# Blocks of 512 tokens with single buffers in the FFN of an attention and mixture-of-experts kernel, and unread products in its first wait

## The chip, the cores and the metric

The kernel runs on one core of a Trainium2 chip. The metric is device time in microseconds (us), the median of several executions. One further execution was taken by the hardware profiler; the rows below are from it. TensorE does the matmuls (PE in rows, PEld its weight loads), VectorE is DVE, ScalarE is ACT, GpSimd is POOL, SyncE (SP) issues transfers.

## The reference

Linear attention without a softmax, an RMS norm, a mixture of eight experts with one expert for each token, and a bilinear FFN over all 2304 tokens:

```python
kv = np.einsum('bhsd,bhse->bhde', k, v)            # (4, 8, 64, 64)
out = np.einsum('bhsd,bhde->bhse', q, kv)          # (4, 8, 576, 64)
x = out / sqrt(mean(out * out) + 1e-6) * g_norm    # as (2304, 512)
e = argmax(x @ w_gate)                             # top-1 of 8, capacity 576
y = relu(x @ w1[e]) @ w2[e]                        # 512 -> 1024 -> 512
out = gate * y
a = out @ w1_ ; b = out @ w2_                      # 512 -> 1024 each
result = ((a * b) @ w3) @ w_out                    # 1024 -> 1024 -> 512
```

## The kernel before

**Precision.** Every large product is done with operands split into a rounded part "hi" and a remainder "lo". PASSES lists three matmuls, hi x hi, hi x lo and lo x hi, so a product over 512 rows (KC = 4 chunks of 128) takes 12 matmuls and one over 1024 rows takes 24.

**Attention and gate** (to about 86 us). For each of four batches: kv, the products with q, norm, gate logits, and the ranks of tokens within their expert. At its end `emit_gather(0)` has GpSimd fetch the rows of the first expert in three indirect transfers (`rows`, L752). `emit_xt(0, j)` then transposes the j-th 128 rows on TensorE (xtp, L764), ScalarE writes the hi part of `xt` (L766), VectorE the lo part (L769).

**Experts** (to about 375 us). Eight experts in the order of their size, NR[r] = 376 down to 272 columns each. For each of 8 groups m of hidden units, `emit_mm1` does 12 matmuls hp (L815) and `emit_mm2` 12 matmuls yp (L832). The weights are "pieces": 512 KB each, loaded by SyncE, split by ScalarE (L731) and VectorE (L740) into a ring of seven buffers. Beside this the FFN's matrices are converted, and w34 = w3 @ w_out is computed, eight groups of 24 matmuls of 512 columns (w34p, L685; its stationary operand lies in the ring too), stored to DRAM and loaded again. The result of the experts lies in `yb`, columns by tokens; the first 256 of the first expert are in `ys0`.

**FFN** (to the end). NBLK = 9 blocks of BLK = 256 tokens. For each of 8 groups f of 128 hidden units `bilinear` does 12 matmuls for a and 12 for b. Its stationary operand is a piece of the FFN's first matrices: pieces 8E + 2 (f // 2) + s, of which seven lie in the ring and the last (f = 6 and 7, s = 1) in the pool u7, on the right side of SBUF. The moving operand is y, split into hi and lo: block 0 reads `ys0`, odd blocks `ys1`, even ones `ys0` again. ScalarE copies a out of PSUM (`at`, L873), VectorE multiplies it with b (`gt`, L875), ScalarE rounds (g hi, L876), VectorE takes the remainder (g lo, L877). g has two buffers. `project` takes 128 tokens: 24 matmuls of 512 columns, stationary g, moving w34 (zp, L884); ScalarE scales the result by the gate (`ob`, L890), GpSimd scatters it to DRAM (L891). The loop runs one block ahead: in block i, after f = 2 and after f = 5, it projects 128 tokens of block i - 1. `emit_ysplit(i + 1)` comes after f = 4 of block i (L858 on ScalarE, L859 on VectorE). In block 0 the last pieces are still split, and from f = 4 on the four slices of w34 (`split_w34`, L1119 and L1120).

The order on each engine is that of the program text; nothing reorders it. A tile that is allocated again waits until all that read the last one are done. PSUM is used as four single banks (`one_bank`) and two pairs (`two_banks`, `pair`).

Of the kernel before, what the change touches and what calls it, by code (L numbers as in the profile page):

```python
# [24 lines left out]
def kernel(  # L25
# [40 lines left out]

    NR = [376, 342, 324, 310, 300, 292, 286, 272]
    Y0 = 256
    BLK = 256
    NBLK = NT // BLK  # L70
    YB = sum(NR) - Y0
    KC = D // 128
    NM = F // 128
# [684 lines left out]
    def emit_xt(r, j):  # L758
        n = min(128, NR[r] - 128 * j)
        if j == 0:  # L760
            xt[r] = xt_p.tile([128, 2, KC, NR[r]], F32R, tag="xt", name="xt")
        p = one_bank("xtp", [128, KC, 128])
        for c in range(KC):
            PE_.transpose(p[:, c, 0:n], rows[r][0:n, j, 128 * c:128 * c + 128], ident[0:n, 0:n])  # L764
        s = slice(128 * j, 128 * j + n)
        ACT.activation(out=xt[r][:, 0, :, s], in_=p[:, :, 0:n], func=AF.Copy, scale=g2[:, 0:1])  # L766

        def lo():
            DVE.scalar_tensor_tensor(  # L769
                out=xt[r][:, 1, :, s], in0=p[:, :, 0:n], scalar=g2[:, 0:1],  # L770
                in1=xt[r][:, 0, :, s].bitcast(F32), op0=ALU.mult, op1=ALU.subtract,
            )
            DVE.tensor_tensor(  # L773
                out=mt[0:n, r, j, 1:2], in0=rows[r][0:n, j, D:D + 1], in1=keep3[0:n, j:j + 1], op=ALU.mult
            )

        return lo
# [72 lines left out]
                ACT.activation(out=yb[:, 2 * i:2 * i + 2, ds(o[0], n)], in_=p[:, :, 0:n], func=AF.Copy)  # L850


    gs = {}

    def emit_ysplit(i):
        src = yb[:, :, BLK * (i - 1):BLK * i]
        t = ysb[i % 2]
        ACT.copy(t[:, 0], src)  # L858
        DVE.tensor_tensor(out=t[:, 1], in0=src, in1=t[:, 0].bitcast(F32), op=ALU.subtract)  # L859

    def bilinear(y, g, f, n, ab_p, p):
        for s in range(2):
            w = piece[8 * E + 2 * (f // 2) + s].rearrange("p s (c f) -> p s c f", c=KC)
            i = 0
            for c in range(KC):
                for a, b_ in PASSES:
                    PE_.matmul(  # L867
                        p[s][:, 0:n], lhsT=w[:, a, c, 128 * (f % 2):128 * (f % 2) + 128], rhs=y[:, b_, c, 0:n],
                        start=(i == 0), stop=(i == 3 * KC - 1),
                    )  # L870
# [5 lines left out]
        ACT.copy(g[:, 0, f, 0:n], gt)  # L876
        DVE.tensor_tensor(out=g[:, 1, f, 0:n], in0=gt, in1=g[:, 0, f, 0:n].bitcast(F32), op=ALU.subtract)  # L877

    def project(g, t, scale, ids, dst, ob_p):
        p = one_bank("zp")  # L880
# [68 lines left out]
    with tc.manual_schedule():  # L949
# [47 lines left out]
        ys0 = y_p.tile([128, 2, KC, BLK], F32R, name="ys0")  # L997
# [107 lines left out]
        close(cv_cm)  # L1105
        u7_cm, u7_p = pool("u7", "right")
        g_cm, g_p = pool("g", "right", 2)
        ysb = [ys0, g_p.tile([128, 2, KC, BLK], F32R, bufs=1, name="ys1")]
# [12 lines left out]

        oviews = dram_disjoint_views(out, NT // 128)
        over = emit_over()
        for i in range(NBLK + 1):
            if i < NBLK:
                gs[i] = g_p.tile([128, 2, NG, BLK], F32R, tag="g", name="g")
            for f in range(NG):
                if i < NBLK:
                    if i == 0:
                        for _ in range((2, 2, 1)[f] if f < 3 else 0):  # L1130
                            split_hi()
                            weave(split_lo())
                    ab = [one_bank("a"), one_bank("b")] if i == 0 else pair()
                    bilinear(ysb[i % 2], gs[i], f, BLK, g_p, ab)
                    if i == 0 and f >= 4:
                        split_w34(f - 4)
                        if f == 4:
                            DVE.tensor_copy(ids, cm[:, :, 0])
                    if i == 0 and 2 <= f < 6:
                        load_w34(f - 2)  # L1140
# [11 lines left out]
    with tc.tile_pool(name="ovf", bufs=1, side="right") as ov_p, \  # L1152
            tc.tile_pool(name="ovl", bufs=1, side="left") as ol_p:
        n = nc.values_load(n_over[0:1, 0:1], min_val=0, max_val=NE)
        with tc.For_i(0, n, 1) as i:
# [77 lines left out]
                DVE.tensor_tensor(out=yo[:, 1, c, :], in0=p, in1=yo[:, 0, c, :].bitcast(F32), op=ALU.subtract)  # L1233
            go = ov_p.tile([128, 2, NG, 128], F32R, name="go")
            for f in range(NG):
                bilinear(yo, go, f, 128, ov_p, pair())
            project(go, 0, om[:, 1:2], idi[:, 0:1], out, ov_p)
    close(u7_cm)
    close(ring_cm)
# [60 lines left out]
```

## Time and profile before

| | us |
|---|---|
| three timed executions | 702.26, 702.43, 704.74 |
| median | 702.43 |
| the profiled execution, its own time | 698.08 |
| its span, first to last instruction | 696.4 |
| TensorE busy | 643.1 (92%) |
| VectorE busy | 387.4 (56%) |
| ScalarE busy | 303.2 (44%) |

All sums are made against the profiled execution. A row of the timeline gives the start, the duration, engine, line, operation, output <- inputs, shape, and how many instructions are merged in it; in brackets the idle time of the engine before it and what ended it. Matmuls are pipelined: the duration of a group holds the drain of its last one, so the pace is better read from the start of one group to the start of the next. PEclk is the granted clock as a share of 2.4 GHz; 0.50 is the 1.2 GHz level.

### The profile page before, as it was taken

The numbers are of one execution on the slowest core, as the hardware profiler recorded it, in microseconds if no ns is written. First come the engines' busy times: TensorE is split into PE (matmuls) and PEld (weight loads), VectorE is DVE, ScalarE is ACT, GpSimd is POOL, SyncE is SP. The second block draws the span as 40 slices with busy tenths as digits, with TensorE's granted clock in tenths as the row PEclk, the third lists the DMA queues.
The fourth block names the chain that finished last, engine by engine and source line by source line (L and its number), as shares of the span: only waits on it lengthen the run. The fifth ranks groups of instructions, "written<-read, shape, count | busy, mean of one in ns | idle before, by whom it ended". The sixth has DMA issues, their size and how long they took to land.

```text
span 696.4 us, 12049 instructions
## 1 busy us (share of the span) xinstructions
PE 643.1 (92%) x4617; PEld 602.5 (87%) x4617; DVE 387.4 (56%) x873; ACT 303.2 (44%) x554; POOL 88.4 (13%) x147
## 2 busy tenths in 40 slices
PE   4987269999999999999999999999999999999993
PEld 3876169998999999998999999999999999999982
DVE  2278968989989988888993644221212221212110
ACT  0546368665756665656653522222222222222210
POOL 4035530202020200211000000000000000000001
PEclk9989569999999999999999999999999999999998
DMA  7992577978899897898864400000000000000000
GB/s 271 336 369 72 182 246 195 216 211 200 300 234 275 212 284 201 273 235 251 210 232 122 140 16 16 16 16 16 16 16 16 15 16 16 16 16 16 16 16 33
DMA packets 35344, 96.78 MB, mean 139 GB/s; under 512 B 8894, under 2 KB 9918, under 8 KB 35282
## 3 DMA queue, kind: packets, MB, share of 16 engines
q1 hardware_dynamic: 28978, 82.48, 40.2%
q0 software_dynamic: 5328, 13.44, 6.5%
q8 instruction: 38, 0.62, 0.4%
q14 instruction: 24, 0.20, 0.1%
q10 hardware_dynamic: 976, 0.04, 0.1%
HBM read 80.15 MB, written 15.79 MB: 138 GB/s over the span
## 4 chain that ended last, share of the span: by engine, by line
issue 41%; PE 36%; DVE 10%; DMA 6%; POOL 3%; ACT 2%; POOLq 0%; SPq 0%; ACTq 0%; DVEq 0%
PE hp L815 13%; PE yp L832 12%; PE w34p L685 6%; POOL out_dram L891 3%; PE op L406 2%; DMA raw<-in_w_out_dram 1%; DVE piece L740 1%; PE xtp L764 1%; PE kv L386 1%; DMA rows<-xbuf,gidx 1%; DMA vin<-in_v_dram 1%; DVE ssq L417 1%; DMA raw<-in_w_dram 1%; DVE one L561 1%; DMA raw<-ud 1%
## 5 line engine op out<-in xcount | busy, mean ns | idle before, releaser
L867 PEld LDWEIGHTS ab<-ys,piece 128*128 128x128 f32 x1536 | 186.0, 190 | 1.4
L867 PE MATMUL ab<-ys,piece 128*128 128x256 f32 x1536 | 186.4, 282 | 0.0
L815 PE MATMUL hp<-xt,piece 128*128 128x376 f32 (+7 forms) x768 | 124.6, 312 | 2.8 <-DVE h L799 1.1
L832 PE MATMUL yp<-h,piece 128*128 128x376 f32 (+7 forms) x768 | 121.1, 306 | 0.9 <-ACT yb L850 0.9
L875 DVE TENSOR_TENSOR gt<-at,ab 128x256 f32<-128x256 f32 x64 | 26.9, 420 | 170.4 <-ACT at L873 170.4
L815 PEld LDWEIGHTS hp<-xt,piece 128*128 128x128 f32 x768 | 114.5, 191 | 4.2 <-DVE h L799 1.4
L832 PEld LDWEIGHTS yp<-h,piece 128*128 128x128 f32 x768 | 113.1, 188 | 1.7 <-ACT yb L850 1.4
L884 PE MATMUL zp<-w,g 128*128 128x512 f32 x432 | 103.8, 396 | 0.0
L740 DVE TENSOR_TENSOR piece<-raw,piece 128x512 fp32r<-128x512 f32 x144 | 92.6, 685 | 15.1 <-ACT piece L731 14.4
L884 PEld LDWEIGHTS zp<-w,g 128*128 128x128 f32 x432 | 80.2, 188 | 18.2
L731 ACT CAST piece<-raw 128x1024 fp32r<-128x1024 f32 x72 | 75.2, 1047 | 2.0 <-DMA raw<-ud 1.5
L873 ACT COPY at<-ab 128x256 f32<-128x256 f32 x64 | 23.9, 373 | 103.3 <-PE ab L867 103.3
L891 POOL DMA_INDIRECT out_dram<-ob,ids x18 | 17.8, 988 | 288.8 <-ACT ob L890 284.1
L877 DVE TENSOR_TENSOR g<-gt,g 128x256 fp32r<-128x256 f32 x72 | 30.7, 426 | 34.0 <-ACT g L876 34.0
L876 ACT CAST g<-gt 128x256 fp32r<-128x256 f32 x72 | 29.3, 407 | 42.7 <-DVE gt L875 42.7
L193 ACT ACTIVATE x<-raw 128x512 f32<-128x512 f32 x40 | 27.1, 679 | 45.3 <-DMA raw<-in_u_dram 13.5
L890 ACT ACTIVATE ob<-zp,cm 128x512 f32<-128x512 f32 x18 | 12.4, 688 | 76.5 <-PE zp L884 71.5
L685 PE MATMUL w34p<-wo,w3t 128*128 128x512 f32 x192 | 45.1, 390 | 0.0
L685 PEld LDWEIGHTS w34p<-wo,w3t 128*128 128x128 f32 x192 | 35.6, 188 | 7.1
L785 POOL DMA_DIRECT2D cmeta<-mt x24 | 13.7, 574 | 202.0 <-DVE mt L773 119.9
L795 ACT ACTIVATE h<-hp 128x376 fp32r<-128x376 f32 (+7 forms) x64 | 27.6, 431 | 26.6 <-PE hp L815 26.6
L799 DVE SCALAR_TENSOR_TENSOR h<-hp,h 128x376 fp32r<-128x376 f32 (+7 forms) x64 | 30.6, 478 | 8.5 <-ACT h L795 8.4
(169 smaller groups left out, 611.9 us busy)
## 6 DMA issues: line engine op xcount, KB each, us to landing
raw<-in_w_dram SPq DMA_DIRECT2D x80, 512.0 KB, 5.8
raw<-in_u_dram SPq DMA_DIRECT2D x16, 512.0 KB, 6.5
qin<-in_q_dram SPq DMA_DIRECT2D x8, 576.0 KB, 7.0
kin<-in_k_dram SPq DMA_DIRECT2D x8, 512.0 KB, 7.3
vin<-in_v_dram SPq DMA_DIRECT2D x8, 512.0 KB, 7.2
raw<-in_w_out_dram SPq DMA_DIRECT2D x8, 512.0 KB, 9.1
ud<-x SPq DMA_DIRECT2D x16, 256.0 KB, 5.0
raw<-ud SPq DMA_DIRECT2D x8, 512.0 KB, 4.2
```

What stands on the lines that cost most here:

```text
L685: PE_.matmul(p, lhsT=t[:, a, c, :], rhs=wo_t[:, c // 2, b_, 512 * (c % 2):512 * (c % 2) + 512], start=(i == 0), stop=(i == 3 * NG - 1),)
L731: ACT.copy(piece[i][:, 0, :], t)
L740: DVE.tensor_tensor(out=s[:, 1, c], in0=t[:, c], in1=s[:, 0, c].bitcast(F32), op=ALU.subtract)
L795: ACT.activation(out=t[:, 0, 0:n], in_=p[:, 0:n], func=AF.Relu)
L799: DVE.scalar_tensor_tensor(out=t[:, 1, 0:n], in0=p[:, 0:n], scalar=0.0, in1=t[:, 0, 0:n].bitcast(F32), op0=ALU.max, op1=ALU.subtract,)
L815: PE_.matmul(p[:, 0:n], lhsT=w[:, a, c, 128 * (m % 2):128 * (m % 2) + 128], rhs=xt[r][:, b_, c, :], start=(i == 0), stop=(i == 3 * KC - 1),)
L832: PE_.matmul(yps[r][c // 2][:, c % 2, 0:n], lhsT=w[:, a, m % 2, c, :], rhs=t[:, b_, 0:n], start=(m == 0 and i == 0), stop=(m == NM - 1 and ...
L867: PE_.matmul(p[s][:, 0:n], lhsT=w[:, a, c, 128 * (f % 2):128 * (f % 2) + 128], rhs=y[:, b_, c, 0:n], start=(i == 0), stop=(i == 3 * KC - 1),)
L876: ACT.copy(g[:, 0, f, 0:n], gt)
L877: DVE.tensor_tensor(out=g[:, 1, f, 0:n], in0=gt, in1=g[:, 0, f, 0:n].bitcast(F32), op=ALU.subtract)
L884: PE_.matmul(p, lhsT=g[:, a, f, 128 * t:128 * t + 128], rhs=w34[:, f, b_, :], start=(i == 0), stop=(i == 3 * NG - 1),)
L891: POOL.indirect_dma_start(out=dst, out_offset=bass.IndirectOffsetOnAxis(ap=ids, axis=0), in_=ob, in_offset=None, bounds_check=NT - 1, oob_ ...
```

## The change

1. BLK is 512: block 0 keeps its 256 tokens (Y0), then come four blocks of 512. `bilinear` issues one matmul of 512 columns where two of 256 stood.
2. g has one buffer (of twice the size). y's hi part is the one tile `ysh`; the lo part `ysl` shares the buffer of `ys0` (tag "ys"). The product of a and b overwrites `at`.
3. The loop no longer runs a block ahead: a block's eight f, then the split of the next block's y (in two halves), then this block's projections, two for block 0 and four for each other.
4. Before the first `emit_xt`, 18 bf16 matmuls of 512 columns are issued whose result `warm` nothing reads, and 4 and 8 more before the second and third.

```diff
-    BLK = 256
-    NBLK = NT // BLK
+    BLK = 512
+    NBLK = 1 + (NT - Y0) // BLK
...
     def emit_ysplit(i):
-        src = yb[:, :, BLK * (i - 1):BLK * i]
-        t = ysb[i % 2]
-        ACT.copy(t[:, 0], src)
-        DVE.tensor_tensor(out=t[:, 1], in0=src, in1=t[:, 0].bitcast(F32), op=ALU.subtract)
+        ysl = y_p.tile([128, KC, BLK], F32R, tag="ys", name="ysl")
+        for c in (slice(0, 2), slice(2, 4)):
+            src = yb[:, c, BLK * (i - 1):BLK * i]
+            ACT.copy(ysh[:, c], src)
+            DVE.tensor_tensor(out=ysl[:, c], in0=src, in1=ysh[:, c].bitcast(F32), op=ALU.subtract)
+        return ysh, ysl
...
-        gt = ab_p.tile([128, n], F32, tag="gt", name="gt")
-        DVE.tensor_tensor(out=gt, in0=at, in1=p[1][:, 0:n], op=ALU.mult)
+        DVE.tensor_tensor(out=at, in0=at, in1=p[1][:, 0:n], op=ALU.mult)
...
+        warm_p = one_bank("warm")
+        def warm(n):
+            for _ in range(n):
+                PE_.matmul(
+                    warm_p.rearrange("p (a b) -> p a b", a=4), lhsT=pos_o,
+                    rhs=pos_o.unsqueeze(1).to_broadcast([128, 4, 128]), start=True, stop=True,
+                )
+        warm(18)
...
         xl = [emit_xt(0, 0)]
         split_hi()
         for j in (1, 2):
+            warm(4 * j)
             xl.append(emit_xt(0, j))
...
-        for i in range(NBLK + 1):
...
-                    if f == 4 and i + 1 < NBLK:
-                        emit_ysplit(i + 1)
...
-                if i and f in (2, 5):
-                    t = 2 * (i - 1) + (f == 5)
-                    project(gs[i - 1], t % 2, cm[:, t, 1:2], ids[:, t:t + 1], oviews[t], g_p)
+        for i in range(NBLK):
+            w = BLK if i else Y0
+            g = g_p.tile([128, 2, NG, BLK], F32R, tag="g", bufs=1, name="g")
...
+            if i + 1 < NBLK:
+                ysb = emit_ysplit(i + 1)
+            for j in range(w // 128):
+                project(g, j, cm[:, t, 1:2], ids[:, t:t + 1], oviews[t], g_p)
+                t += 1
```

TensorE at the gathers of the first expert, before (xtp are the transposes, hp the first expert's matmuls):

```order
L764 MATMUL xtp<-ident,rows 128x128 x8
L764 MATMUL xtp<-ident,rows 128x120 x4
L815 MATMUL hp<-xt,piece 128x376 x36
L832 MATMUL yp<-h,piece 128x376 x12
L815 MATMUL hp<-xt,piece 128x376 x12
```

The same place now, each LDWEIGHTS and MATMUL warm standing for 18, 4 and 8 such pairs:

```order
L589 MATMUL idp<-idr,one 128x16
L1001 LDWEIGHTS pos_o
L1001 MATMUL warm<-pos_o 128x512
...
L764 MATMUL xtp<-ident,rows 128x128 x4
L1001 LDWEIGHTS pos_o
...
L764 MATMUL xtp<-ident,rows 128x128 x4
L1001 LDWEIGHTS pos_o
...
L764 MATMUL xtp<-ident,rows 128x120 x4
L815 MATMUL hp<-xt,piece 128x376 x36
```

The unread products stand in front of each transpose on TensorE's queue; what follows the transposes is as before.

TensorE from the last group of block 0 on, before (ys_1103 is ys0, ys_4627 is ys1; ab a pair of banks, zp a projection):

```order
L867 MATMUL b<-ys_1103,piece 128x256 x12
L867 MATMUL ab<-ys_4627,piece 128x256 x72
L884 MATMUL zp<-w_4628,g 128x512 x24
L867 MATMUL ab<-ys_4627,piece 128x256 x72
L884 MATMUL zp<-w_4628,g 128x512 x24
L867 MATMUL ab<-ys_4627,piece 128x256 x48
L867 MATMUL ab<-ys_1103,piece 128x256 x72
```

And now (ys_1122 is ys0; L883 is the line of the projection):

```order
L867 MATMUL b<-ys_1122,piece 128x256 x12
L883 MATMUL zp<-w_4659,g 128x512 x48
L867 MATMUL ab<-ysh,piece 128x512
L867 MATMUL ab<-ysl,piece 128x512
L867 MATMUL ab<-ysh,piece 128x512 x2
...
L883 MATMUL zp<-w_4659,g 128x512 x96
```

The projections of a block follow its last bilinear group directly, two in block 0 and four after each later block; before, six or five groups of 24 stood between them.

ScalarE in the same place, before (w_4628 are the slices of w34, ys_4627 the split of block 1's y):

```order
L1119 CAST w_4628<-w34f 128x2x512
L858 CAST ys_4627<-yb 128x1024
L873 COPY at<-a 128x256
L876 CAST g<-gt 128x256
L1119 CAST w_4628<-w34f 128x2x512
...
L873 COPY at<-ab 128x256
L876 CAST g<-gt 128x256
L890 ACTIVATE ob<-zp,cm 128x512
```

And now, from the last slice of w34 on (L1131):

```order
L873 COPY at<-a 128x256
L875 CAST g<-at 128x256
L1131 CAST w_4659<-w34f 128x2x512
L857 CAST ysh<-yb 128x1024 x2
L889 ACTIVATE ob<-zp,cm 128x512 x2
L873 COPY at<-ab 128x512
L875 CAST g<-at 128x512
```

The split of block 1's y has moved from between the first two slices of w34 to behind the last, ahead of the first output; VectorE's counterparts move likewise.

## Rows read from the trace of the kernel before

**Rows 1.** The page: busy us, share of the span and instructions of each engine.

```profile
PE 643.1 (92%) x4617; PEld 602.5 (87%) x4617; DVE 387.4 (56%) x873; ACT 303.2 (44%) x554; POOL 88.4 (13%) x147
```

**Rows 2.** Stretches: length, busy us (instructions) of each engine, PEclk, DMA share, GB/s.

```profile
60.00:75.00 15.00, 8.05 (x77) 6.52 (x76) 13.68 (x47) 8.29 (x22) 8.27 (x10) 0.77 0.34 121
...
80.00:90.00 10.00, 3.04 (x23) 2.19 (x23) 8.74 (x35) 1.69 (x2) 3.20 (x3) 0.50 0.59 175
...
95.00:99.00 4.00, 4.00 (x13) 4.00 (x14) 3.75 (x7) 3.40 (x5) 2.28 (x2) 0.51 0.20 39
...
150.00:200.00 50.00, 49.14 (x302) 46.22 (x301) 47.97 (x101) 30.80 (x51) 6.17 (x8) 1.00 0.86 226
500.00:600.00 100.00, 100.00 (x700) 93.42 (x700) 23.52 (x51) 25.32 (x56) 4.92 (x6) 1.00 0.04 14
```

**Rows 3.** Groups of TensorE by shape: count, busy us, mean ns, idle before.

```profile
L867 PE MATMUL ab<-ys,piece 128*128 128x256 f32 x1536 | 186.4, 282 | 0.0
L884 PE MATMUL zp<-w,g 128*128 128x512 f32 x432 | 103.8, 396 | 0.0
```

**Rows 4.** Timeline of TensorE in the FFN, one block and its neighbours.

```profile
516.22 8.79 PE L867 MATMUL ab<-ys,piece 128*128 128x256 f32 x72
524.85 5.78 PE L884 MATMUL zp<-w,g 128*128 128x512 f32 x24
530.46 14.47 PE L867 MATMUL ab<-ys,piece 128*128 128x256 f32 x120
544.77 5.54 PE L884 MATMUL zp<-w,g 128*128 128x512 f32 x23
```

**Rows 5.** Chain that ended last, in order of time: start us, us, what.

```profile
109.88 2.07 PE hp L815 x12
...
165.41 5.46 PE w34p L685 x24
...
361.12 1.50 PE hp L815 x12
```

**Rows 6.** Timeline of TensorE, the end of block 0.

```profile
393.70 1.60 PE L867 MATMUL a<-ys,piece 128*128 128x256 f32 x12
...
397.98 1.57 PE L867 MATMUL b<-ys,piece 128*128 128x256 f32 x12
399.38 8.80 PE L867 MATMUL ab<-ys,piece 128*128 128x256 f32 x72
```

**Rows 7.** Timeline of ScalarE and VectorE in the FFN: split of y, output.

```profile
489.19 1.05 ACT L858 CAST ys<-yb 128x1024 fp32r<-128x1024 f32 x1
...
490.27 1.23 DVE L859 TENSOR_TENSOR ys<-yb,ys 128x1024 fp32r<-128x1024 f32 x1 [0.53 <-ACT ys L858]
...
496.46 0.69 ACT L890 ACTIVATE ob<-zp,cm 128x512 f32<-128x512 f32 x1 [4.19 <-PE zp L884]
```

**Rows 8.** Timeline of VectorE, the last slice of w34.

```profile
403.21 1.23 DVE L1120 TENSOR_TENSOR w<-w34f,w 128x1024 fp32r<-128x1024 f32 x1 [0.52 <-ACT w L1119]
```

**Rows 9.** Timeline of TensorE, its last projections.

```profile
672.88 11.41 PE L884 MATMUL zp<-w,g 128*128 128x512 f32 x48
```

**Rows 10.** Timeline of TensorE around the first gathers.

```profile
69.02 0.19 PE L526 MATMUL pp<-oh,tri 128*128 128x40 bf16 x1 [2.27 <-DVE oh L512]
...
71.87 1.27 PE L589 MATMUL idp<-idr,one 128*128 128x16 bf16 x15 [2.44 <-DVE one L561]
...
79.98 1.63 PE L589 MATMUL idp<-idr,one 128*128 128x16 bf16 x15 [1.58 <-DVE one L561]
86.40 1.11 PE L764 MATMUL xtp<-ident,rows 128*128 128x128 f32 x4 [4.79 <-DMA rows<-xbuf,gidx]
...
93.10 1.03 PE L764 MATMUL xtp<-ident,rows 120*128 120x120 f32 x4 [2.73 <-DMA rows<-xbuf,gidx]
94.94 8.26 PE L815 MATMUL hp<-xt,piece 128*128 128x376 f32 x36 [0.80 <-ACT xt L766]
...
109.28 0.60 PE L764 MATMUL xtp<-ident,rows 128*128 128x128 f32 x4
```

More of the change, by code (lines that the diff above doesn't have):

```diff
@@ L867, in bilinear @@
                     PE_.matmul(
-                        p[s][:, 0:n], lhsT=w[:, a, c, 128 * (f % 2):128 * (f % 2) + 128], rhs=y[:, b_, c, 0:n],
+                        p[s][:, 0:n], lhsT=w[:, a, c, 128 * (f % 2):128 * (f % 2) + 128], rhs=y[b_][:, c, 0:n],
                         start=(i == 0), stop=(i == 3 * KC - 1),
@@ L873, in bilinear @@
         ACT.copy(at, p[0][:, 0:n])
-        gt = ab_p.tile([128, n], F32, tag="gt", name="gt")
-        DVE.tensor_tensor(out=gt, in0=at, in1=p[1][:, 0:n], op=ALU.mult)
-        ACT.copy(g[:, 0, f, 0:n], gt)
-        DVE.tensor_tensor(out=g[:, 1, f, 0:n], in0=gt, in1=g[:, 0, f, 0:n].bitcast(F32), op=ALU.subtract)
+        DVE.tensor_tensor(out=at, in0=at, in1=p[1][:, 0:n], op=ALU.mult)
+        ACT.copy(g[:, 0, f, 0:n], at)
+        DVE.tensor_tensor(out=g[:, 1, f, 0:n], in0=at, in1=g[:, 0, f, 0:n].bitcast(F32), op=ALU.subtract)
     def project(g, t, scale, ids, dst, ob_p):
@@ L996 @@
         h_cm, h_p = pool("h", "right", 2)
-        ys0 = y_p.tile([128, 2, KC, BLK], F32R, name="ys0")
+        warm_p = one_bank("warm")
[6 more added lines that the diff above has]
+        warm(18)
+        ys0 = y_p.tile([128, 2, KC, Y0], F32R, tag="ys", name="ys0")
         yb = y_p.tile([128, KC, YB], F32, name="yb")
@@ L1107 @@
         g_cm, g_p = pool("g", "right", 2)
-        ysb = [ys0, g_p.tile([128, 2, KC, BLK], F32R, bufs=1, name="ys1")]
+        ysh = g_p.tile([128, KC, BLK], F32R, bufs=1, name="ysh")
+        ysb = ys0[:, 0], ys0[:, 1]
         w34 = wp.tile([128, NG, 2, D], F32R, tag="w", name="w34")
@@ L1123 @@
         over = emit_over()
-        for i in range(NBLK + 1):
-            if i < NBLK:
-                gs[i] = g_p.tile([128, 2, NG, BLK], F32R, tag="g", name="g")
+        t = 0
+        for i in range(NBLK):
+            w = BLK if i else Y0
+            g = g_p.tile([128, 2, NG, BLK], F32R, tag="g", bufs=1, name="g")
             for f in range(NG):
[L1128 to L1140, printed above, removed]
-                    if f == 4 and i + 1 < NBLK:
-                        emit_ysplit(i + 1)
+                if i == 0:
+                    for _ in range((2, 2, 1)[f] if f < 3 else 0):
+                        split_hi()
+                        weave(split_lo())
+                bilinear(ysb, g, f, w, g_p, pair() if i else [one_bank("a"), one_bank("b")])
+                if i == 0 and f >= 4:
+                    split_w34(f - 4)
+                    if f == 4:
+                        DVE.tensor_copy(ids, cm[:, :, 0])
+                if i == 0 and 2 <= f < 6:
+                    load_w34(f - 2)
                 if i == 1:
                     next(over, None)
-                if i and f in (2, 5):
-                    t = 2 * (i - 1) + (f == 5)
-                    project(gs[i - 1], t % 2, cm[:, t, 1:2], ids[:, t:t + 1], oviews[t], g_p)
+            if i + 1 < NBLK:
[3 more added lines that the diff above has]
+                t += 1
+            for _ in over if i == 1 else ():
+                pass
         close(g_cm)
@@ L1235 @@
             for f in range(NG):
-                bilinear(yo, go, f, 128, ov_p, pair())
+                bilinear((yo[:, 0], yo[:, 1]), go, f, 128, ov_p, pair())
             project(go, 0, om[:, 1:2], idi[:, 0:1], out, ov_p)
```

1 line of the change is left out of this document (removed).

## Prediction

> **What bounds the kernel now.** I read first the engines' shares. TensorE is busy 643.1 us, 92% of the span [rows 1], so the question is what each of its matmuls costs and where it still waits. Then the table by stretches [rows 2]: from 500 to 600 us, which stands for the whole end of the program, TensorE is busy 100.00 of 100 us at full clock, VectorE 23.52 and ScalarE 25.32. In that stage nothing is waited for; only fewer or cheaper matmuls can shorten it. From 150 to 200 us the expert stage is nearly balanced instead: TensorE 49.14, VectorE 47.97 of 50. And from 80 to 90 us TensorE is busy 3.04 of 10 us, at a granted clock of 0.50 (the 1.2 GHz level); it stays at 0.51 from 95 to 99, where it is already busy without a break. So the change touches two places: the FFN stage, where each matmul counts, and the gap ahead of the first expert, where TensorE waits and is slow afterwards.
>
> **The pace of the FFN's matmuls.** The stage issues 1536 matmuls of 256 columns in blocks 1 to 8 and 432 projections of 512 [rows 3]. Starts give their pace [rows 4]: 72 of 256 columns take 524.85 - 516.22 = 8.63 us, 120 take 544.77 - 530.46 = 14.31 us, together 22.94 / 192 = 119.5 ns. At 2.4 GHz 256 columns are 106.7 ns of streaming, so 12.8 ns of each are not streaming. After the change the same columns go through as 768 matmuls of 512; two of the old ones, 239.0 ns, become one. What does one of 512 cost? The trace has two answers. The projections: 530.46 - 524.85 = 5.61 us for 24, 233.8 ns [rows 4]. The product w34 = w3 @ w_out in the expert stage: 5.46 us for 24, 227.5 ns [rows 5]. At 233.8 the stage gains 768 x 5.2 ns = 4.0 us, at 227.5 it gains 768 x 11.5 ns = 8.8 us.
>
> Which is nearer? 227.5 is 213.3 of streaming plus 14.2, and 119.5 is 106.7 plus 12.8: the FFN's old matmuls and w34's look like the same thing, a nearly fixed cost per matmul. The projections look like a cost per column, 233.8 / 213.3 = 1.10, and so do the first expert's matmuls, 2.07 us for 12 of 376 columns, 172.5 / 156.7 = 1.10, and the last one's, 1.50 us for 12 of 272, 125.0 / 113.3 = 1.10 [rows 5]. In block 0 a group of 12 spans 1.60 us, but the group whose weights are the last piece (which lies in the pool u7, on the other side of SBUF from the ring) only 1.57 [rows 6]: less the last one's own 0.28 [rows 3], 11 steps of 120 and of 117.3 ns, and 117.3 / 106.7 is 1.10 again. So one group in eight (f = 6 and 7, second factor) already goes by the column and the other seven by the matmul. The ring's weights stay where they are, so I keep that split: 7/8 at 227.5 and 1/8 at 233.8, mean 228.3. Gain: 768 x (239.0 - 228.3) = **8.2 us**.
>
> The rows show 12.8 ns beyond the streaming of 256 columns, and 14.2 or 20.5 beyond that of 512 [rows 4, 5]. The Trainium skill ("TensorE: Matmul & The Clock Gate", section "Back-to-back issue gap") gives columns / 2.4 plus about 2.5 ns for a warm stream. By that rule one large matmul for two saves only 2.5 ns, so the stage would gain 768 x 2.5 = 1.9 us instead of 8.2. The trace disagrees with its size, so it stays a rival.
>
> **What the larger block asks of the other engines: nothing that shows.** Per f TensorE now needs 24 x 0.228 = 5.5 us. The eviction is a chain of four steps: copy of a to `at`, times b, rounding to hi, remainder lo, by turns on ScalarE and VectorE. At 512 columns a ScalarE step is bounded by the output eviction, 0.69 us, a VectorE step by the subtraction over 1024 columns, 1.23 us [rows 7]: at most 3.8 us, and two pairs of banks give it two f, 11 us. That the product now overwrites `at` adds no wait. The single g costs nothing, because its next writer waits for bilinear matmuls that TensorE itself issues after the block's last projection. What had two buffers and now has one is y: the split of the next block can start only when the block's last bilinear matmul has read ysh and ysl. It is two casts and two subtractions of 1024 columns, 1.05 and 1.23 us each [rows 7]; the second cast runs beside the first subtraction, so the chain is 1.05 + 2.46 = 3.5 us. It lies under 2 projections after block 0 (48 x 0.234 = 11.2 us) and under 4 at the three later boundaries (22.5 us). On ScalarE's queue the casts stand ahead of the first output eviction, which is ready only 5.6 us after the block's end. Cost 0 while this cover stands; without it 3.5 us at each of four boundaries.
>
> After block 0 there is one tight place. The projection now follows f = 7 at once; before, 72 matmuls lay between. It reads w34's slices in order; the last slice's remainder is needed at its 20th matmul, 19 x 0.234 = 4.4 us after block 0's end at 399.27 to 399.38, so at 403.8. In the trace that remainder ends at 403.21 + 1.23 = 404.44 [rows 8]. That would be a stall of 0.7 us. But the ys cast (1.05) and subtraction (1.23) [rows 7] that stand between the w34 splits on both queues are moved behind them, which draws the chain forward by some 0.8 us, somewhat less than the cast. I take a stall of 0.2 us, bounds 0 and 0.7: **-0.2 us**.
>
> SyncE's order is the same; on GpSimd the iota moves behind two output scatters, whose reader on VectorE comes only in block 1. The end is unchanged: the last 48 projections already ran back to back (11.41 us) [rows 9]. The drain behind them stays.
>
> **The unread products.** TensorE ends its gate work at 79.98 + 1.63 = 81.6 and waits for three gathers, the first until 86.40, the third until 93.10 [rows 10]. Into it go 18, 4 and 8 bf16 products of 512 columns. From 95 to 99, at half clock, 13 matmuls of 376 columns took 4.00 us, 308 ns [rows 2]; by columns a 512 one takes 0.42 us there and about 0.23 at full clock, which is an estimate from these rows.
> - Gain at most: 36 matmuls of 376 took 8.26 us [rows 10]; at 172.5 ns [rows 5] they take 6.2, so 2.1 us, and the third transpose 1.03 instead of 0.60 us [rows 10]: 2.5 us in all.
> - But behind the last product TensorE waits again for the third gather and then for the ScalarE copy of xt (0.80 us). The clock, full until then, was at 0.50 after waits of 2.27 and 2.44 us at 69 and 72 us (mean 0.77 from 60 to 75) [rows 2, 10]. It may well fall again before the experts begin; then only the transpose and perhaps 0.5 us remain.
> - Loss at most: if the clock rises late, 18 x 0.42 = 7.6 us run to 89.2, the first transposes are late by 2.8, and 12 more products and two transposes push the third to some 94.0, 0.9 us behind its gather.
> - What is gained runs into a stage in which VectorE is busy 47.97 of 50 us [rows 2]; part of it can be waited away there.
>
> Between -0.9 and +2.5 I take **+1.0 us**, near the transpose plus a half.
>
> **Sum.** 8.2 + 1.0 - 0.2 = 9.0 us. Against the profiled execution (698.08 us, span 696.4) that is 689.1. The median of the three timed runs, 702.43, lies 4.35 above it; nothing in the change touches that difference, so I put the sum on the median: 693.4 us.
>
> **The rivals.**
> 1. *By the column.* All 512-column matmuls go at the projections' 233.8 ns. For: same stage, same columns, and the experts' 1.10. Against: seven groups of eight of the old FFN do not. Gain 4.0 + 0.8: 697.6 us.
> 2. *Only a small fixed cost.* A straight line through the experts' rows (172.5 - 125.0) / 104 = 0.457 ns per column, put on from 119.5, gives 236.5 for 512: gain 768 x 2.5 = 1.9, with the rest 2.7: 699.7 us. Against: no row of 512 columns is that slow. The Trainium skill's rule on the gap, above, comes out at the same 1.9 us.
> 3. *The single y is exposed (slower).* If the split waits for the projections too, TensorE stands 3.5 us at each of four boundaries, 14.0 us: 693.4 + 14.0 = 707.4. It decides where the split starts more than 7.7 us late under 11.2 us of projections. Against: neither queue holds a later instruction ahead of it.
> 4. *The products do nothing or harm.* Clock falls again, or the third transpose is 0.9 us late: 693.4 + 1.0 to 1.9, 694.4 to 695.3. This lies inside the forecast's own range.
>
> **How the numbers follow.** Forecast with rival 4: 0.63; rival 1: 0.20; rival 2: 0.08; rival 3: 0.05; 0.04 for a larger gain. The predicted time is the forecast's, 693.4. The low end is 8.8 + 2.5 = 11.3 us of gain, 691.1, rounded down for the runs' spread; the high end takes in rival 1 with costs (4.0 - 0.9 - 0.7 = 2.4 at worst, 700) down to what leaves 2 in 10 out: 690.5 to 699. About 0.5%, 3.5 us, is what a measurement of this kernel can tell from no change. Faster by more (under 698.9): the forecast, the larger gain and most of rival 1, 0.81; within: 0.13; slower: rival 3 and the unknown, 0.06.
>
> **What would show it.** In the profile after: 24 matmuls ab of 512 columns starting about 5.5 us apart from the next 24 (5.6 means rival 1, 5.7 rival 2); TensorE without idle time at the block boundaries (rival 3: 3 to 4 us, released by VectorE's ysl); the first 36 hp in 6.2 us rather than 8.26, or the granted clock at 0.50 again around 95 us; at most some 0.7 us in front of the 20th matmul of the first projection. The forecast is wrong if the ab matmuls' pace is not that of w34p, on which 4.2 of the 9.0 us rest.

## The result, and the profile after

The changed kernel takes 691.93 us (median of four executions; 688.25 to 692.45), the kernel before, timed beside it, 702.94 us. The ratio is 0.983, interval 0.980 to 0.986: faster by 11.0 us. The forecast was 693.4 us, range 690.5 to 699.0. The profiled execution of after took 692.45 us (span 690.9), that of before 698.08 us, so between the two profiled executions only 5.6 of the 11.0 us can be looked for.

The page of after has one line for the engines: busy us, share of the span, instructions. It answers [rows 1]. The stretches answer [rows 2] (length, busy us and instructions of TensorE, its weight loads, VectorE, ScalarE, GpSimd; granted clock; DMA share; GB/s).

```profile
PE 644.3 (93%) x3879; PEld 565.1 (82%) x3879; DVE 377.9 (55%) x809; ACT 293.0 (42%) x490; POOL 89.5 (13%) x147
```

```profile
95.00:99.00 4.00, 3.43 (x13) 3.37 (x14) 3.43 (x7) 4.00 (x6) 1.65 (x2) 0.70 0.26 103
...
500.00:600.00 100.00, 100.00 (x432) 80.69 (x431) 22.69 (x30) 22.88 (x35) 4.92 (x5) 1.00 0.04 14
```

From 500 to 600 us TensorE is busy without a gap, as before, with 432 matmuls instead of 700. The clock at the start of the first expert is still not full throughout in this execution: 0.70 over these 4 us, beside 0.51.

The FFN as TensorE's timeline shows it (start us, busy us, what, count): the projections of block 0, the first bilinear matmul of block 1, its projections, the first of block 2, and the last projections of the program. These answer [rows 4, 9].

```profile
399.07 11.40 PE L883 MATMUL zp<-w,g 128*128 128x512 f32 x48
410.31 0.40 PE L867 MATMUL ab<-ysh,piece 128*128 128x512 f32 x1
...
454.87 22.64 PE L883 MATMUL zp<-w,g 128*128 128x512 f32 x96
477.35 0.40 PE L867 MATMUL ab<-ysh,piece 128*128 128x512 f32 x1
...
655.99 22.65 PE L883 MATMUL zp<-w,g 128*128 128x512 f32 x96
```

A block's 192 bilinear matmuls take 454.87 - 410.31 = 44.56 us, **232.1 ns** each; 24 take 5.57 us. The 96 projections take 477.35 - 454.87 = 22.48 us, 234.2 ns each, where [rows 4] gave 233.8. So the new matmuls lie between the two prices of the prediction (227.5 and 233.8), nearer to the dearer one. Grouped by shape (count, busy us, mean ns of one, idle before), which answers [rows 3], a difference by tile shows:

```profile
L867 PE MATMUL ab<-ysh,piece 128*128 128x512 f32 x512 | 161.7, 396 | 0.0
L883 PE MATMUL zp<-w,g 128*128 128x512 f32 x432 | 102.0, 396 | 0.0
L867 PE MATMUL ab<-ysl,piece 128*128 128x512 f32 x256 | 100.0, 391 | 0.0
L685 PE MATMUL w34p<-wo,w3t 128*128 128x512 f32 x192 | 45.2, 391 | 0.0
```

The mean includes the time for which one matmul overlaps the next, so it is no pace; but matmuls with ysl in motion look like those of w34 (391), and those with ysh in motion like the projections (396).

The end of block 0, on VectorE and ScalarE (in brackets idle time before and what ended it), answers [rows 6, 8]:

```profile
401.79 1.23 DVE L1132 TENSOR_TENSOR w<-w34f,w 128x1024 fp32r<-128x1024 f32 x1 [0.52 <-ACT w L1131]
402.93 2.36 DVE L858 TENSOR_TENSOR ysl<-yb,ysh 128x1024 fp32r<-128x1024 f32 x2
```

```profile
401.66 1.99 ACT L857 CAST ysh<-yb 128x1024 fp32r<-128x1024 f32 x2
404.89 0.69 ACT L889 ACTIVATE ob<-zp,cm 128x512 f32<-128x512 f32 x1 [1.24 <-PE zp L883]
```

The last remainder of w34 ends at 403.02, 3.95 us after block 0's end; before it was 404.44 - 399.38 = 5.06 us after it, so it is 1.1 us earlier. The 20th matmul of the first projection is due at 399.07 + 4.4 = 403.5: nothing waits. The split of y ends at 405.29, five us ahead of the first matmul of block 1.

TensorE around the first gathers answers [rows 10]:

```profile
82.38 6.00 PE L1001 MATMUL warm<-pos_o 128*128 128x512 bf16 x18
88.22 0.60 PE L764 MATMUL xtp<-ident,rows 128*128 128x128 f32 x4
...
90.01 1.89 PE L1001 MATMUL warm<-pos_o 128*128 128x512 bf16 x8
94.17 0.61 PE L764 MATMUL xtp<-ident,rows 120*128 120x120 f32 x4 [2.27 <-DMA rows<-xbuf,gidx]
95.57 8.01 PE L815 MATMUL hp<-xt,piece 128*128 128x376 f32 x36 [0.80 <-ACT xt L766]
```

The products raise the clock: the transposes take 0.60 and 0.61 us instead of 1.11 and 1.03. Then TensorE waits 2.27 us for the third gather, the clock falls, and the first 36 matmuls take 8.01 us, hardly less than 8.26.

One stretch of the path is used below. From the end of block 0 to the end of the last projection TensorE never waits in any kernel: 672.88 + 11.41 - 399.38 = 284.9 us before [rows 6, 9], 655.99 + 22.65 - 399.07 = 279.6 after. Three profiled executions of the FFN of after (two of after, one without products) give 279.56 to 279.57 us for it, so this stretch is known to some 0.01 us, while the start of the FFN moves by several us from one execution to the next.

### The profile page after: what moved, and what is told of

The parts are those of the page before. It is cut to its first block, busy times and chain, and to the rows that moved or that the text cites. A ratio compares the mean times of both kernels' runs of the same rounds, so it can differ in the third digit from the quotient of the medians.

```text
span 690.9 us, 10405 instructions
## 1 busy us (share of the span) xinstructions
PE 644.3 (93%) x3879; PEld 565.1 (82%) x3879; DVE 377.9 (55%) x809; ACT 293.0 (42%) x490; POOL 89.5 (13%) x147
## 4 chain that ended last, share of the span: by engine, by line
PE 40%; issue 39%; DVE 9%; DMA 5%; POOL 3%; ACT 2%; POOLq 0%; SPq 0%; ACTq 0%; DVEq 0%
PE hp L815 13%; PE yp L832 12%; PE w34p L685 6%; POOL out_dram L890 3%; PE op L406 2%; PE a L867 2%; PE b L867 2%; DMA raw<-in_w_dram 1%; PE kv L386 1%; DMA raw<-in_u_dram 1%; DMA rows<-xbuf,gidx 1%; PE xtp L764 1%; DMA vin<-in_v_dram 1%; DVE piece L740 1%; DVE ssq L417 1%
## 5 line engine op out<-in xcount | busy, mean ns | idle before, releaser
L867 PE MATMUL ab<-ysh,piece 128*128 128x512 f32 x512 | 161.7, 396 | 0.0
L874 DVE TENSOR_TENSOR at<-at,ab 128x512 f32<-128x512 f32 x32 | 22.1, 689 | 175.6 <-ACT at L873 175.6
L867 PEld LDWEIGHTS ab<-ysh,piece 128*128 128x128 f32 x512 | 96.0, 187 | 22.3
L883 PE MATMUL zp<-w,g 128*128 128x512 f32 x432 | 102.0, 396 | 0.0
L867 PE MATMUL ab<-ysl,piece 128*128 128x512 f32 x256 | 100.0, 391 | 0.0
L883 PEld LDWEIGHTS zp<-w,g 128*128 128x128 f32 x432 | 81.3, 188 | 19.7
L873 ACT COPY at<-ab 128x512 f32<-128x512 f32 x32 | 18.8, 588 | 120.5 <-PE ab L867 120.5
L867 PEld LDWEIGHTS ab<-ysl,piece 128*128 128x128 f32 x256 | 48.1, 188 | 11.9
L785 POOL DMA_DIRECT2D cmeta<-mt x24 | 13.8, 578 | 204.3 <-DVE mt L773 135.1
L876 DVE TENSOR_TENSOR g<-at,g 128x512 fp32r<-128x512 f32 (+1 forms) x40 | 25.6, 639 | 25.8 <-ACT g L875 25.8
L875 ACT CAST g<-at 128x512 fp32r<-128x512 f32 (+1 forms) x40 | 23.2, 579 | 33.4 <-DVE at L874 33.4
```

The lines of the kernel that those rows point to most:

```text
L867: PE_.matmul(p[s][:, 0:n], lhsT=w[:, a, c, 128 * (f % 2):128 * (f % 2) + 128], rhs=y[b_][:, c, 0:n], start=(i == 0), stop=(i == 3 * KC - 1),)
L874: DVE.tensor_tensor(out=at, in0=at, in1=p[1][:, 0:n], op=ALU.mult)
L875: ACT.copy(g[:, 0, f, 0:n], at)
L876: DVE.tensor_tensor(out=g[:, 1, f, 0:n], in0=at, in1=g[:, 0, f, 0:n].bitcast(F32), op=ALU.subtract)
L883: PE_.matmul(p, lhsT=g[:, a, f, 128 * t:128 * t + 128], rhs=w34[:, f, b_, :], start=(i == 0), stop=(i == 3 * NG - 1),)
```

## Experiments: the two halves of the change

**The products alone.** The kernel before, with nothing of the FFN changed:

```diff
+        warm_p = one_bank("warm")
+        ... warm(n) as in the change
+        warm(18)
...
         for j in (1, 2):
+            warm(4 * j)
             xl.append(emit_xt(0, j))
```

> The kernel before with the unread products alone. The timed runs moved by 11.0 us (702.94 to 691.93), the two profiled executions only by 5.6 us (698.08 to 692.45). Theory A (the products are worth what the profile after shows at the first expert: 36 matmuls in 8.01 instead of 8.26 us): at most 1 us faster than before, and the granted clock falls to 0.50 again before the first expert. Theory B (the timed runs of before lost more at half clock than its profiled one, and the products give that back): 4 to 6 us faster than before.

Measured: 697.54 us beside 702.88, ratio 0.994 (0.991 to 0.996): 4.5 us by the ratio, 2.6 to 6.4. In this execution the clock was full from the products on:

```profile
93.26 0.60 PE L764 MATMUL xtp<-ident,rows 120*128 120x120 f32 x4 [0.81 <-DMA rows<-xbuf,gidx]
94.66 6.47 PE L815 MATMUL hp<-xt,piece 128*128 128x376 f32 x36 [0.80 <-ACT xt L766]
```

36 matmuls take 6.47 us instead of 8.26, and the matmuls behind them start at 100.96 instead of 103.03. The trace has 2.1 us of gain there, about half of what the time has; the rest of the 4.7 us between the two profiled executions (698.08 and 693.40) is 1.9 in the expert stage and 0.6 in block 0, which move that much from one execution to the next anyway. Theory A falls. The size of theory B fits, but its reason does not: the 21 executions of the kernel before that were timed here have granted clocks of 0.963 to 0.970, median 0.967, and the profiled one has 0.968. So they lost hardly more at half clock than the profiled one: 0.001 of the clock is 0.7 us of 700.

**The FFN alone.** The changed kernel without the two calls of warm and its definition.

> The change without the unread products. By the two profiles the FFN stage gains 768 x (239.0 - 232.1) = 5.3 us, and block 0 some 0.7. Theory A: all the rest is here as well, so as fast as the whole change, about 10 us faster than before. Theory B: about 6 us faster than before, 4 to 5 us slower than the whole change.

Measured: 695.81 us, ratio 0.990 (0.986 to 0.994), 6.9 us by the ratio. The stretch from block 0 to the end is 279.57 us, as after.

**After, unchanged, beside them.**

> The whole change once more, on the same chip as the three others, so that they can be compared with it: 10 to 11 us faster than before if the first timing holds, 5 to 6 if the profiled executions are the measure.

Measured: 691.81 us, ratio 0.987 (0.982 to 0.991). So the medians put the products at 4.0 us (695.81 to 691.81), but the intervals of the two ratios overlap, and the two profiled executions are equal (693.93 and 694.08). Here the clock stayed up; the waits ahead of the second and third transposes were 1.33 and 0.19 us, and 36 hp took 6.47 us. The 2.1 us gained by their end (101.13 beside 103.20) were mostly waited away: from there to the FFN TensorE stood 5.3 us, mostly for VectorE and ScalarE, instead of 3.4 without products.

## Experiments: what sets the pace

The pace of 232.1 ns needed a cause. What differs between ysh and ysl, and between the projections and w34, is where the tiles start in SBUF. In the program as built, the ring's pieces, w34, wo, ys0 and ysl start at multiples of 512 bytes in each partition; ysh and g start 96 bytes beyond one (157792 and 165984), and the last piece, in u7, 480 bytes beyond one. The same holds of g and u7's piece in the kernel before.

**ysh and g moved down to multiples of 512.** After, with 480 unused bytes in u7's pool and 128 more in a small buffer of g's pool; the instructions of the FFN are the same:

```diff
-I32: g_p.tile([1, 64], I32, bufs=1, name="oi")
+I32: g_p.tile([1, 96], I32, bufs=1, name="oi")
...
         u7_cm, u7_p = pool("u7", "right")
+        DVE.memset(u7_p.tile([128, 120], F32, name="pad"), 0.0)
```

> The change, with ysh and g moved down by 608 bytes in each partition so that they start at a multiple of 512 bytes (they started 96 beyond one); the last piece in u7 stays where it was, 480 beyond one. A pad tile and a larger oi do it; one small memset is added. Theory P (the pace depends on where an operand starts: all operands at 512 give 227, any one off it gives 234): ab 227 in the groups of the ring's pieces and 234 in those of the last piece, zp 227 instead of 234.2, together 768 x 4.2 + 432 x 7.2 = 6.3 us faster than the whole change. Rival Q (the pace belongs to the work itself: two moving tiles by turns, or ScalarE and VectorE reading PSUM): ab stays at 232, zp at 234, no difference.

Measured: 686.78 us, ratio 0.979 (0.976 to 0.982), 5.0 us under after as timed beside it. TensorE's timeline, the same five places as above:

```profile
397.95 11.06 PE L883 MATMUL zp<-w,g 128*128 128x512 f32 x48
408.85 0.39 PE L867 MATMUL ab<-ysh,piece 128*128 128x512 f32 x1
...
452.53 21.92 PE L883 MATMUL zp<-w,g 128*128 128x512 f32 x96
474.29 0.39 PE L867 MATMUL ab<-ysh,piece 128*128 128x512 f32 x1
...
648.85 21.92 PE L883 MATMUL zp<-w,g 128*128 128x512 f32 x96
```

A block's bilinear matmuls take 43.68 us, 227.5 ns each, and the projections 21.76 / 96 = 226.7 ns. By shape all three groups now have w34's mean:

```profile
L867 PE MATMUL ab<-ysh,piece 128*128 128x512 f32 x512 | 158.6, 390 | 0.0
L867 PE MATMUL ab<-ysl,piece 128*128 128x512 f32 x256 | 99.8, 390 | 0.0
L883 PE MATMUL zp<-w,g 128*128 128x512 f32 x432 | 98.7, 389 | 0.0
```

The piece in u7, which was not moved, is a control within the run. Starts that lie 12 matmuls apart, the last two groups of f in block 1:

```profile
441.26 0.61 PE L867 MATMUL ab<-ysh,piece 128*128 128x512 f32 x2
...
443.98 0.63 PE L867 MATMUL ab<-ysh,piece 128*128 128x512 f32 x2
...
446.78 0.61 PE L867 MATMUL ab<-ysh,piece 128*128 128x512 f32 x2
...
449.50 0.63 PE L867 MATMUL ab<-ysh,piece 128*128 128x512 f32 x2
```

2.72, 2.80 and 2.72 us: 226.7 ns with the ring's piece, 233.3 with u7's, 226.7 again. Where the stationary operand starts counts as much as where the moving one does. The buffers of `at` and the output lie in the same pool and moved along with g, but TensorE reads neither, and the last kernel below, in which of these tiles only u7's piece moves further, changes these groups alone.

**How far must they be moved?** After with 32, 480 and 352 bytes ahead of ysh and g, so that they start 64, 128 and 256 bytes beyond a multiple of 512 (the diff is that of 64; the pad has 120 and 88 elements in the others). These runs and all further ones were made on another chip than the four above, one on which the kernel before takes 697.1 to 697.8 us instead of 702.9; so ratios can be compared with those above, times can't.

```diff
         u7_cm, u7_p = pool("u7", "right")
+        DVE.memset(u7_p.tile([128, 8], F32, name="pad"), 0.0)
```

> The changed kernel with 32 bytes put ahead of ysh and g instead of 608: they then start 64 bytes beyond a multiple of 512 (a multiple of 64; before it was 96 beyond, no multiple of 64). Theory 64 (the rows of 64 bytes decide): ab 226.7 ns and zp 227 ns as in the run with the aligned tiles, 5 us off the changed kernel, 686.8. Theory 512 (only a multiple of 512, or at least of 128, will do): ab 232 and zp 234 as in the changed kernel, 691.9.

> The changed kernel with 480 bytes ahead of ysh and g: they start 128 bytes beyond a multiple of 512. If a multiple of 128 is enough: ab 226.7 ns with the ring's pieces, zp 227.5, ratio about 0.979. If not: ab 232 to 234, zp 233 to 234, ratio 0.985 to 0.99.

> The changed kernel with 352 bytes ahead of ysh and g: they start 256 bytes beyond a multiple of 512. At 64 beyond, ab went at 233.6 ns and zp at 233.3, at a multiple of 512 at 226.7 and 227.5. If a multiple of 256 is enough: ab 226.7 ns with the ring's pieces, zp 227.5, and a ratio to the kernel before of about 0.979. If only 512 will do: ab 232 to 234, zp 233 to 234, ratio 0.985 to 0.99.

Timelines of block 1, at 64, 128 and 256 bytes beyond:

```profile
408.49 0.39 PE L867 MATMUL ab<-ysh,piece 128*128 128x512 f32 x1
...
453.21 22.56 PE L883 MATMUL zp<-w,g 128*128 128x512 f32 x96
475.61 0.39 PE L867 MATMUL ab<-ysh,piece 128*128 128x512 f32 x1
```

```profile
414.60 0.40 PE L867 MATMUL ab<-ysh,piece 128*128 128x512 f32 x1
...
458.60 22.46 PE L883 MATMUL zp<-w,g 128*128 128x512 f32 x96
480.90 0.39 PE L867 MATMUL ab<-ysh,piece 128*128 128x512 f32 x1
```

```profile
406.77 0.39 PE L867 MATMUL ab<-ysh,piece 128*128 128x512 f32 x1
...
450.45 21.92 PE L883 MATMUL zp<-w,g 128*128 128x512 f32 x96
472.21 0.39 PE L867 MATMUL ab<-ysh,piece 128*128 128x512 f32 x1
```

| ysh and g start at | ab, ns | zp, ns | block 0's end to the last zp, us | ratio of the times |
|---|---|---|---|---|
| 64 beyond 512 | 232.9 | 233.3 | 279.83 | 0.990 (0.988 to 0.992) |
| 96 (after) | 232.1 | 234.2 | 279.57 | 0.983 (0.980 to 0.986) |
| 128 | 229.2 | 232.3 | 276.65 | 0.985 (0.982 to 0.987) |
| 256 | 227.5 | 226.7 | 272.82 | 0.980 (0.976 to 0.983) |
| multiple of 512 | 227.5 | 226.7 | 272.82 | 0.979 (0.976 to 0.982) |

Of the starts tried, a multiple of 256 is enough and nothing less is; at 128 part of the price goes. The theory that 64 is enough falls: it is no better than 96. The ratios, taken beside different runs of the kernel before, move by more than the stretch explains (0.990 at 64, 0.983 and 0.987 at 96, with almost the same stretch); the stretch is the sharper measure.

**The same places with the small blocks.** The kernel before, with the two edits of 480 and 128 bytes:

> The kernel before (blocks of 256, two buffers of y and g, no products) with the tiles ys1 and both g moved down by 608 bytes to multiples of 512. Separates the place of the tiles from the size of the block. If the place matters for matmuls of 512 columns and, by the rows of before (120 ns with the ring's pieces for either y, aligned or not), not for those of 256: the 432 projections go from 233.8 to 227 ns, 2.9 us, the 1536 ab stay at 119.5 ns, and the time is 700.0 us beside 702.9. If the place were worth as much without the larger block as with it (5 us): 697.9. If nothing: 702.9.

```profile
513.10 8.79 PE L867 MATMUL ab<-ys,piece 128*128 128x256 f32 x72
521.73 5.63 PE L884 MATMUL zp<-w,g 128*128 128x512 f32 x24
527.20 14.47 PE L867 MATMUL ab<-ys,piece 128*128 128x256 f32 x120
541.51 3.82 PE L884 MATMUL zp<-w,g 128*128 128x512 f32 x16
```

Measured: 695.24 us beside 697.09, ratio 0.997 (0.995 to 0.999). The 192 of 256 columns take 8.63 + 14.31 = 22.94 us, as in [rows 4] to the hundredth; the 24 projections take 5.47 instead of 5.61. So the place of an operand costs matmuls of 512 columns 6 to 7 ns and those of 256 nothing. The stretch from block 0 to the end falls by 2.80 us, all of it the projections' (432 x 6 ns = 2.6).

**Without products, aligned, and with them once more.** The aligned kernel without warm, and the same aligned kernel as above:

> The run with aligned tiles without the unread products. With the run that has them, of the same call, this gives the products' worth a third time (4.0 and 5.3 us so far, where the traces explain 2.2, as the first 36 matmuls of the first expert end 2.1 us earlier and a microsecond there was worth one at the end). If the products are worth what the traces show: 2 us more than the run with aligned tiles and products, a ratio 0.003 higher. If they are worth 4 to 5: a ratio 0.006 to 0.007 higher. Against the small blocks with aligned tiles (0.9974) the larger block alone should give 768 x (239.0 - 227.5) = 8.8 us and 0.9 us at the end of block 0: a ratio of about 0.984.

> The kernel with aligned tiles and products, once more, for the comparison with the same kernel without the products on one chip: ratio 0.979 as in the first call.

Measured: 684.42 us, ratio 0.980 (0.978 to 0.983), and 683.45 us, ratio 0.980 (0.977 to 0.983). The stretch is 272.82 us in both. Beside the aligned small blocks (282.10) the larger block alone is worth 9.3 us where every operand of the ring and of y lies well, beside 5.3 where ysh does not. The products are worth 1.0 us here by the medians, which the two ratios can't tell from nothing. The ratio of 0.984 that was expected without products was missed by 0.004.

## Experiments: what the start of the experts is worth

**Thirty more products ahead of the first expert.** The aligned kernel with

```diff
             warm(4 * j)
             xl.append(emit_xt(0, j))
+        warm(30)
```

> The run with the aligned tiles (ysh and g moved down to a multiple of 512 bytes) and 30 more unread products of 512 columns between the third transpose and the first expert's matmuls. Its own stretches gave about 0.217 us for one such product at full clock, so the first expert starts 30 x 0.217 = 6.5 us later. The question is what a microsecond at the start of the experts is worth at the end, since the products of the change gained 4 to 5 us where the clock in the trace explains 2.2. Theory S (one for one: from there TensorE is the path, and the rest of the gain lies in what the loads make of the expert stage in one execution and another): 6.5 us longer than the run with the aligned tiles, 693.3. Rival T (a late start costs more than itself, since loads of weights fall behind with it): 9 us or more, over 696. Rival U (the expert stage waits for VectorE or the loads and takes up the delay): 3 us or less, under 690.

```profile
95.18 6.64 PE L1001 MATMUL warm<-pos_o 128*128 128x512 bf16 x30
101.47 6.53 PE L815 MATMUL hp<-xt,piece 128*128 128x376 f32 x36
107.84 2.27 PE L832 MATMUL yp<-h,piece 128*128 128x376 f32 x12
```

The first expert begins at 101.47 instead of 94.44 (its gathers came 0.8 us later too, the products cost 6.29), its first 36 matmuls end at 107.84 instead of 100.74, the last projection of the program at 677.92 instead of 670.77: 7.03, 7.10 and 7.15 us. By time: 690.02 us, ratio 0.989 (0.987 to 0.991) where the aligned kernel has 0.979, some 7 us. The bounds of the theories in us were set beside a kernel before of 702.9 us, so the ratios decide; with their intervals the difference is 4 to 10 us. That excludes that the experts take the delay up (3 us or less), and by time alone just touches a cost of 9 us or more. The trace says one for one.

**Everything that helped.** The aligned kernel, with its 480 bytes in u7's pool now *behind* the piece instead of ahead of ysh and g, which moves the piece's start to a multiple of 512 and leaves ysh and g where they were; and 14 products instead of 8, with 3 behind the third transpose:

```diff
-            piece[i] = u7_p.tile([128, 2, 1024], F32R, name="piece") if i == NP - 1 else ring("piece")
+            piece[i] = u7_p.tile([128, 2168], F32R, name="piece")[:, 0:2048].rearrange("p (s x) -> p s x", s=2) if i == NP - 1 else ring("piece")
...
-            warm(4 * j)
+            warm((4, 14)[j - 1])
             xl.append(emit_xt(0, j))
+        warm(3)
```

> The run with the aligned tiles, and two things more: the ring's last piece, the one in u7, gets 480 bytes behind it, so that it starts at a multiple of 512 too; and 14 products instead of 8 stand ahead of the third transpose and 3 more behind it. The piece: 96 of the 768 matmuls of 512 columns go at 227 instead of 233 ns, 0.6 us. The products: in one profiled execution of three the clock was down again ahead of the first expert, which cost some 2 us there; if that happens in many executions, the median falls by up to 1.5 us; if the clock is up in most, by nothing, and a third transpose that comes late would cost up to 0.5 us. Expected 684.5 to 686.5 us beside 686.8 of the run with aligned tiles alone; in the trace all ab of 512 columns at 226.7 to 227.5 ns.

```profile
406.69 0.39 PE L867 MATMUL ab<-ysh,piece 128*128 128x512 f32 x1
...
450.21 21.92 PE L883 MATMUL zp<-w,g 128*128 128x512 f32 x96
471.97 0.39 PE L867 MATMUL ab<-ysh,piece 128*128 128x512 f32 x1
```

Measured: 682.16 us beside 697.09, ratio 0.979 (0.976 to 0.981): the same as the aligned kernel's. The time lies under the 684.5 to 686.5 expected, which were worked out from a run on the first chip. The trace has the expected 0.6 us: 43.52 us per block, 226.7 ns for every bilinear matmul, and 272.19 us for the stretch. It is the best of the versions by the trace, some 7.4 us under after on that stretch, and level with the aligned one by time.

## Why the prediction was right, and where not

**Direction, size and range were right; the sum was not made of the right terms.** The forecast of 9.0 us was 8.2 for the pace, 1.0 for the products, -0.2 for a stall. The traces give 5.3, about 1, and 0.

**The pace: the mechanism was right, the term mis-sized.** 768 matmuls of 512 columns in place of 1536 of 256 gain by their pace, not by anything else: 768 x (239.0 - 232.1) = 5.3 us, which is the whole fall of the stretch (284.90 to 279.57). By the prediction's own sign the term failed: 24 matmuls start 5.57 us apart, nearer to the 5.6 of rival 1 than to the 5.5 of the forecast, and their pace is not w34p's. The step that failed is "The ring's weights stay where they are, so I keep that split". It had seen that u7's piece goes by another law than the ring's, and had even named where that piece lies; but it took the place of the *weights* for the whole cause. The pace hangs on where either operand starts. In ysh the change put 512 of the 768 moving operands on a bad start, and there the price by the column (1.10 of the streaming) comes back. The projections' rows had said so: their moving w34 lies well, their stationary g does not, and they cost 233.8 [rows 4]. The working treated 227.5 and 233.8 as two laws for two kinds of work, when they are one matmul with well and badly placed operands; with ysh and g moved, both go at 226.7 (the bilinear ones with the ring's pieces). Whether the 1.10 of the experts' matmuls has the same cause was not tried; as built, their moving operand xt starts 480 or 224 bytes beyond a multiple of 512.

**Rival 1** (by the column, 4.0 us) was nearer to this term than the forecast: 5.3 us lie between its 4.0 and the forecast's 8.2, at three tenths of the way. **Rival 2** (a small fixed cost, 1.9 us) falls: even on the bad start the term is 5.3. The best pace measured for these f32 matmuls is 226.7 ns for 512 columns, 13.3 beyond the streaming, and 120.0 for 256, 13.3 too. The unread bf16 products go faster: 30 take 6.64 us and 8 take 1.89, so one takes 216 ns at full clock. The Trainium skill ("TensorE: Matmul & The Clock Gate", section "Back-to-back issue gap") gives 2.5 ns beyond the streaming, and calls it the gap of an isolated matmul, where the prediction has "a warm stream". The trace agrees for the bf16 products and not for the f32 matmuls.

**The other engines: right.** No idle time at any block boundary; the four-step eviction and the single g cost nothing. **Rival 3** (the single y exposed) falls: the split after block 0 ends at 405.29, block 1 begins at 410.31.

**The stall after block 0: 0, not 0.2.** Measured from block 0's end, the split's chain was drawn forward by 1.1 us, not by 0.8. (Before, three groups of 24, 72 matmuls, stood between a block's last group and its first projection and three more ahead of its second [rows 4], not "six or five" as the section on the change has it.) The length of block 0 itself, 23.94 before and 23.22 after, shows no gain of the change: with the same FFN it was 24.66 and 23.95 in two other executions.

**The products: the working held, its size is only bounded by the times.** "It may well fall again before the experts begin" happened in two of eight profiled executions with these 18, 4 and 8 products: in after (behind the 2.27 us wait above) and in the run with 128 bytes, where the second gather came late:

```profile
93.03 0.63 PE L764 MATMUL xtp<-ident,rows 128*128 128x128 f32 x4 [3.03 <-DMA rows<-xbuf,gidx]
93.50 3.50 PE L1001 MATMUL warm<-pos_o 128*128 128x512 bf16 x8
96.80 0.69 PE L764 MATMUL xtp<-ident,rows 120*128 120x120 f32 x4
98.29 6.46 PE L815 MATMUL hp<-xt,piece 128*128 128x376 f32 x36 [0.80 <-issue]
```

There the eight products started 0.43 us apart, but for the first two, and stood ahead of the third transpose, a loss of the kind that the prediction described, though it came from a clock that fell again and not from one that rose late. In the other six the first 36 matmuls took 6.44 to 6.47 us. They ended at 101.7 on average over the eight, at 102.6 over the four profiled executions without products (103.03, 103.20, 102.09, 102.02): 0.9 us, and in the run with thirty more products a microsecond there was worth one at the end. By time the products gave 4.5 (2.6 to 6.4), 4.0 and 1.0 us in three pairs, the first two on one chip, the third on another; only the first is clear of the noise. It is more than the traces explain; **what the rest is was not found**, and the third pair does not show it. What the prediction said of a gain that runs into the expert stage ("part of it can be waited away there") is what the profiled execution of after measured again looks like, though such waits differ from one execution to the next in any case.

**What made the total right was partly luck.** The step "nothing in the change touches that difference, so I put the sum on the median" carried 4.35 us between the profiled execution of before and its median over to after; but after's median lies 0.5 *under* its own profiled execution. 698.08 to 692.45 is 5.6 us, and the two traces account for it: 5.3 in the stretch and 0.7 in block 0, less 0.4 because the matmuls behind the first 36 start later (103.42 beside 103.03). The medians show 11.0. The pace term was 2.9 us too large, and the difference between medians and profiled executions made up for it and more. The two kernels with blocks of 512 and no products, too, lie nearly 2 us lower against before than their stretches say: 6.9 us by the ratio (4.3 to 9.6) beside 5.3, and, aligned, 13.8 (12.2 to 15.5) beside 12.1; neither is clear of the noise by itself. This stays open.

What makes whole executions scatter can be read in part. The start of the FFN, in the traces, moves between 371.5 and 379.2 us (380.9 with thirty more products). From the end of the first 36 matmuls to there TensorE stands idle for 1.5 us (the products alone) to 5.3 us (after, measured again), nearly all of it in waits for VectorE and ScalarE; less that, this part takes 269.0 to 270.2 us in all fourteen traces. Why these waits differ was not found.

## What to carry to other kernels

When two rows give two prices for one kind of instruction, ask which property of the operands differs (size, place, role) before calling them two laws: here the start address of a tile in SBUF decided 6 to 7 ns of 227 on each matmul of 512 columns that read it, and a pad of 608 bytes gave more on the stretch (6.7 us) than the whole restructuring (5.3). When a change allocates a new tile, read where it lands. For small effects compare a stretch of the trace in which the bounding engine never waits: it repeats to 0.01 us where whole executions scatter by several.

## What the runs showed of the hardware

- TensorE's pace for fp32 matmuls of 512 columns with a new stationary operand each: 226.7 ns where both operands start at a multiple of 256 bytes, 228.9 to 234.2 where one starts 64, 96, 128 or 480 beyond a multiple of 512, whichever of the two it is (where it is the moving one, the mean of groups in which 8 of 12 matmuls read it). Of 256 columns: 120.0 and 117.0 ns, where the well placed one is the *slower* (in the last kernel, where u7's piece was moved, its groups of block 0 go at 120.0 too).
- bf16 matmuls of 512 columns with one stationary operand, loaded each time: 216 ns at the 2.4 GHz level, 0.43 us at the 1.2 GHz level.
- Waits of 2.27 and 3.03 us for a gather came before a fall of the granted clock from the 2.4 to the 1.2 GHz level, in the middle of a stretch that unread products had brought to full clock.
- A stretch of 280 us with TensorE busy throughout repeats to 0.01 us between executions and between two chips.
